# Hedgehog attention with a SwiGLU gate: the casts of wo bound behind the second query tile's exponentials, and the last wo rows in another buffer

## The chip, the cores and the metric

The kernel runs on one core of one Trainium2 chip. The metric is the device time of one execution in microseconds (us); the median of three runs is given. The engines are called as in the profile: PE is TensorE's matrix multiplication and PEld its weight load, DVE is VectorE, ACT is ScalarE, POOL is GpSimd, and SP is the sync engine, whose queue issues most of the DMAs.

## What is computed

The sequence has S = 2048 rows of D = 576; the attention has H = 32 heads of 18; the feed-forward part has F = 4608 hidden columns. Cut to what matters:

```python
xn = layernorm(x)
q, k, v = heads(xn @ wqkv)
phi(p) = concatenate([softmax(p), softmax(-p)])      # p = q @ w_phi or k @ w_phi, per head: 36 features
kv, z = phi(k)^T v, sum over the rows of phi(k)
o = (phi(q) kv) / (phi(q) z + 1e-6)
s = merged(o) @ wo
g = silu((silu(xn @ w_gate) * (xn @ w_up)) @ w_down)
out = x + s * g
```

## The kernel before, in words

All matrix products run in a reduced 32-bit format, with each fp32 operand split in a high part and a low part: the high part is a cast on ACT (`split` L58, `split_rows` L62), the low part is the source less the cast, on DVE (L59, L63, and L64 for a few leftover rows). A product of two split operands takes three matmuls per piece, high by high, high by low and low by high (`xw` L92, L614).

The program runs in stages. Up to about 230 us of the trace it normalizes x, folds w_phi into the query and key weights, and builds kv and z over the 16 row tiles. Then comes the query stage, 230 to 475 us: 16 query tiles of 128 rows in pairs. Each (`q_tile`, L558 on) multiplies xn by the query weights into a PSUM tile of two banks (`p2`, one buffer for all query tiles, 28 matmuls of 288 columns). `softmax_parts` (L272 to L286) then takes, for each sign, the maximum or minimum per head (L278) and subtracts it (L279), both on DVE; the subtractions are collected in the list `read`, the key tiles' ahead of the query tiles', so that `read[2 * NT + 1]` is the second subtraction of the first query tile and `read[-1]`, when `split_wo` runs, that of the second. ACT takes the two exponentials (L282), DVE the sums (L285). The rest of a query tile is DVE's: the product with z (`ez`, L567), its sum (L569), and small operations that end in scaling `e` in place (L577). `numer` (L579 to L597) transposes the pair of e tiles on PE, splits them and multiplies by kv; `project` (L599 to L620) multiplies by wo, whose halves are `WOH` and `WOL`, and stores s to memory (`so`, L619 and L620).

wo comes in three loads (L531) to buffers that the query stage uses later for something else: `oh`, `ol` and `ez`. `split_wo` (L533 on), which is called once, behind the first pair of query tiles, makes WOH (ACT, L58) and WOL (DVE, L59) of them.

Meanwhile PE also works on "early" tiles of the gate and up product, so that it isn't idle when the attention is: `early_weights` (L100) loads a block of weights (`raw`) and splits it (`wh`, `wl`), `early_tile` (L113) does 14 gate matmuls of 512 columns, a silu on ACT (L119), 14 up matmuls, the product h on DVE (L122) and its store (L123). A pool of PSUM tiles `pe` with two buffers holds both products. `tails` (L540 to L555) prepares the leftover weight rows: a load `tl`, four POOL subtractions (L546 to L549), a cast `th` on ACT (L550), a low part on DVE, and eight stores by POOL.

From 512 us to the end, Strassen-like products of gate and up (L707) alternate with the down products (L832). Their weights are loaded by SP (`ld`, L676), combined by POOL into `ts` and back into `ld` (L694 to L697), cast and made low by `split` into `w`, and stored for a second use (L687). ACT copies a product out of PSUM (`s` from `px`, L736); POOL and DVE combine the hidden tiles (`ha`, `hb`, `h`, L916 to L934), whose split halves `hh` enter the down products with those of the down weights (`dw`, from `rt`, `rb` and `td`).

The order of each engine's instructions is made by a scheduler from the order of the code and its priorities: what stands in `tc.high_priority()` goes first when it can, and `tc.issue_after(x)` puts what is issued in it behind instruction x, but only those of its instructions that run on x's own engine. An engine then works strictly in its order. Buffers of a pool are handed out in turn, so a tile waits until the last reader of the buffer is done.

Of the kernel before, what the change touches and what calls it, by code (L numbers as in the profile page):

```python
# [9 lines left out]
F32 = mybir.dt.float32  # L10
F32R = mybir.dt.float32r
AF = mybir.ActivationFunctionType
# [4 lines left out]
S, D, H, DH, F = 2048, 576, 32, 18, 4608  # L17
P = 128
NT = S // P
# [18 lines left out]
def heads(ap):  # L38
    return ap.rearrange("p (h d) -> p h d", d=DH)
# [7 lines left out]
def gated_hedgehog_kernel(ctx: ExitStack, tc, x, w_qk, w_v, w_phi, wo, w_gu, w_tail, w_down, ident_in, mask_in, out):  # L47
# [5 lines left out]
    nc = tc.nc  # L53
# [3 lines left out]
    def split(hi, lo, src):  # L57
        nc.scalar.copy(hi, src)  # L58
        nc.vector.tensor_sub(lo, src, hi)  # L59
# [22 lines left out]
    def xw(ps, i, j, cols, wh, wl, stationary_x):  # L82
        pairs = []
        for k in range(2):
            b = XB[i][2 * j + k]
            for c in range(2):
                pairs += [(b[:, c, cols], w[:, k, c]) for w in (wh, wl)]
                pairs += [(b[:, 3 + c, cols], wh[:, k, c])]
            pairs += [(b[0:96, 2, cols], wh[0:96, k, 2])]
        for n, (a, b) in enumerate(pairs):  # L90
            l, r = (a, b) if stationary_x else (b, a)
            last = nc.tensor.matmul(ps, l, r, start=n == 0, stop=n == len(pairs) - 1)  # L92
        return last
# [16 lines left out]
            parts.append((hi, lo))  # L110
        return parts

    def early_tile(f, i, parts, js=(0, 1), banks=None):  # L113
        for j in js:
            pg, pu = banks or [eps.tile([P, BT], F32, name="pe") for _ in range(2)]
            xw(pg, i, j, slice(0, BT), *parts[0], False)
            h = epool.tile([P, BT], F32, name="h")
            with tc.high_priority():
                nc.scalar.activation(h, pg, AF.Silu)  # L119
            last = xw(pu, i, j, slice(0, BT), *parts[1], False)  # L120
            with tc.high_priority():
                nc.vector.tensor_mul(h, pu, h)  # L122
            nc.sync.dma_start(h_dram[i, f, :, j * BT:(j + 1) * BT], h)  # L123
        return last

    with ExitStack() as att:
# [9 lines left out]
        with ExitStack() as wst:  # L136
# [129 lines left out]
            kk = kst.enter_context(tc.tile_pool(name="kk", bufs=2, side="right", reuse_waits="tile"))  # L266
# [6 lines left out]
            def softmax_parts(ps, e):  # L273
                m = kk_pool.tile([P, 2, H], F32, name="m", bufs=1)
                p4 = ps[:, :, 0:HALF].rearrange("p a (h d) -> p a h d", d=DH)
                for s, op in enumerate((ALU.max, ALU.min)):
                    m3 = m[:, s].rearrange("p (a h) -> p a h", a=2)
                    nc.vector.tensor_reduce(m3, p4, axis=AX.X, op=op)  # L278
                    read.append(nc.vector.tensor_sub(e[:, s * D:(s + 1) * D].rearrange("p (a h d) -> p a h d", a=2, d=DH),  # L279
                                                     p4, m3.unsqueeze(3).to_broadcast([P, 2, H // 2, DH])))  # L280
                for s in range(2):
                    nc.scalar.activation(e[:, s * D:(s + 1) * D], e[:, s * D:(s + 1) * D], AF.Exp,  # L282
                                         scale=1.0 if s == 0 else -1.0)
                sm = kk_pool.tile([P, 2 * H], F32, name="sm")
                nc.vector.reduce_sum(sm, heads(e), axis=AX.X)  # L285
                return sm  # L286

            kk_pool, read = kk, []

            def kv_step(n, phi, v):  # L290
                for i in range(2 * NG):
# [199 lines left out]
        with ExitStack():  # L491
# [6 lines left out]
            banks = [(i, 4 if i < 2 else 2, GROUPS[2 * i][1]) for i in range(3)]  # L498
# [23 lines left out]
        with ExitStack() as qst:  # L522
            qw = qst.enter_context(tc.tile_pool(name="qw", bufs=1, reuse_waits="tile"))
            qk = qst.enter_context(tc.tile_pool(name="qk", bufs=2, reuse_waits="tile"))
# [1 line left out]
            WOH = qw.tile([GW, NG, D], F32R, name="WOH")  # L526
            WOL = qw.tile([GW, NG, D], F32R, name="WOL")
            wrs = [qk.tile([P, 2, D], F32, name="oh", bufs=1), qk.tile([P, 2, D], F32, name="ol", bufs=1),
                   qk.tile([P, 2, D], F32, name="ez", bufs=1)]
            for g, (o, w) in enumerate(GROUPS):  # L530
                nc.sync.dma_start(wrs[g // 2][0:w, g % 2], wo[o:o + w, :])  # L531

            def split_wo():  # L533
                with tc.issue_after(read[-1].ins):
                    for n, wr in enumerate(wrs):
                        g, w = slice(2 * n, min(2 * n + 2, NG)), GROUPS[2 * n][1]
                        split(WOH[0:w, g], WOL[0:w, g], wr[0:w, 0:min(2, NG - 2 * n)])

            kk_pool = qk
# [99 lines left out]
        for f, halves in [(1, (0,)), (0, (0,))] + [(f, (1, 0)) for f in range(2, EARLY - 1)]:  # L639
            parts = first_weights.pop() if f == 1 else early_weights(f, read[2 * NT + 1] if f == 0 else None)  # L640
            for i in halves:
                early_tile(f, i, parts, (1,) if f == 1 else (0, 1))

    fw = ctx.enter_context(tc.tile_pool(name="fw", bufs=1))
    fp = ctx.enter_context(tc.tile_pool(name="fp", bufs=1, reuse_waits="tile"))
# [74 lines left out]
    def stored(src, fill):  # L720
        h = h_tile()
        for r in range(2):
            nc.sync.dma_start(h[r], src[:, r * BT:(r + 1) * BT])
        for _ in range(2):
            fill()
        return h
# [296 lines left out]
    parts = early_weights(EARLY - 1)  # L1023
# [11 lines left out]
    for i, n, f in units:  # L1035
# [9 lines left out]
        h = stored(h_dram[i, f], fill) if f < EARLY else gate_up(w, xo, fill, f - EARLY + (NF if i else 0))  # L1045
# [60 lines left out]
```

## Time and profile before

| what | value |
|---|---|
| median of 3 runs | 1640.28 us (1638.73 to 1642.0) |
| the profiled execution's own time | 1638.38 us |
| its span, first to last instruction | 1636.6 us, so 1.8 us lie around it |
| mean granted PE clock | 0.998 |
| PE busy in the span | 1604.0 us (98%) |
| DVE, ACT, POOL busy | 71%, 44%, 40% |
| instructions | 25198 |

In a row of the timeline stand the start, the busy time, the engine, the line, the operation, the tiles written and read with their shapes, the count of neighbours that were taken together, and in brackets the engine's idle time before it and what ended that. In the names the buffer numbers are left out. A row of the page's DMA table gives the count, the size of one and the time from issue to landing.

### The profile page before, as it was taken

Reading aid. Unit: us, or ns where it says so; the run is one execution under the profiler, and the core shown is the slowest. Engines: PE = TensorE matmul, PEld = TensorE weight load, DVE = VectorE, ACT = ScalarE, POOL = GpSimd, SP = SyncE. Lnnn points to the kernel's source line nnn. Section 1 sums busy time; section 2 is a strip of 40 time slices with the busy share of each in tenths; the row PEclk is TensorE's granted clock in tenths of the full one; section 3 lists DMA queues with packets and bytes.
Section 4 is the critical chain, followed back from the end, with each engine's and each line's share of the span. In section 5 each row is a group of like instructions: output and inputs, shape, how many; then the busy total and the mean of one; then the engine's idle time right before and its main releaser. Section 6 shows DMA issues by size and latency. Waiting matters only on the chain.

```text
span 1636.6 us, 25198 instructions
## 1 busy us (share of the span) xinstructions
PE 1604.0 (98%) x9385; PEld 1429.7 (87%) x9385; DVE 1168.5 (71%) x1721; ACT 721.9 (44%) x1391; POOL 653.3 (40%) x699
## 2 busy tenths in 40 slices
PE   6999998999999999999999999999999999999998
PEld 5899997999978888888888888888888888888887
DVE  7677768899952678778777778825666766666578
ACT  5533345444432554544444544455433433333334
POOL 3485661333212455455545355313233324133132
PEclk9999999999999999999999999999999999999999
DMA  9622243334248545555554554684454655555444
GB/s 286 206 80 78 85 134 117 117 103 126 67 144 306 184 165 175 179 178 168 177 180 165 175 192 152 224 296 150 136 162 135 199 184 170 172 179 185 140 115 174
DMA packets 121741, 268.46 MB, mean 164 GB/s; under 512 B 12787, under 2 KB 53363, under 8 KB 119827
## 3 DMA queue, kind: packets, MB, share of 16 engines
q1 hardware_dynamic: 106652, 246.49, 45.9%
q0 software_dynamic: 3072, 11.02, 2.4%
q10 hardware_dynamic: 11894, 9.35, 1.8%
q8 instruction: 74, 1.21, 0.3%
q14 instruction: 49, 0.39, 0.1%
HBM read 167.19 MB, written 99.61 MB: 163 GB/s over the span
## 4 chain that ended last, share of the span: by engine, by line
PE 90%; DMA 4%; DVE 3%; POOL 1%; issue 1%; ACT 1%; SPq 0%; ACTq 0%; POOLq 0%; DVEq 0%
PE px L707 24%; PE pd L832 24%; PE pw L707 12%; PE py L707 6%; PE p L92 6%; PE pe L92 5%; PE p L614 4%; PE po L594 2%; PE kvp L294 2%; PE vx L382 1%; PE pt L588 1%; DMA xn<-in_A_x 1%; PE vw L382 1%; DMA s_dram<-so 1%; DMA sraw<-in_A_w_v 1%
## 5 line engine op out<-in xcount | busy, mean ns | idle before, releaser
L832 PEld LDWEIGHTS pd<-dw,hh 128*128 128x128 f32 x3048 | 432.4, 188 | 26.4 <-DVE dw L59 1.7
L832 PE MATMUL pd<-dw,hh 128*128 128x288 f32 x3048 | 448.5, 297 | 4.3 <-DVE dw L59 1.5
L707 PE MATMUL px<-X,w 128*128 128x512 f32 x1488 | 384.3, 393 | 0.0
L707 PEld LDWEIGHTS px<-X,w 128*128 128x128 f32 x1488 | 270.6, 188 | 51.8 <-ACT s L736 2.0
L707 PE MATMUL pw<-X,w 128*128 128x512 f32 x732 | 188.7, 393 | 0.0
L707 PEld LDWEIGHTS pw<-X,w 128*128 128x128 f32 x732 | 137.0, 188 | 30.5
L741 DVE TENSOR_TENSOR s<-pw,s 128x512 f32<-128x512 f32 x124 | 85.1, 688 | 100.0 <-ACT s L736 89.2
L957 DVE TENSOR_TENSOR acc<-pd,acc 128x576 f32<-128x576 f32 x128 | 96.2, 752 | 83.8 <-PE pd L832 83.6
L736 ACT COPY s<-px 128x512 f32<-128x512 f32 x124 | 72.6, 585 | 157.2 <-PE px L707 157.2
L92 PE MATMUL pe<-X,wh 128*128 128x512 f32 (+1 forms) x380 | 121.8, 401 | 5.8 <-ACT h L119 2.9
L59 DVE TENSOR_TENSOR hh<-ha,hh 128x512 fp32r<-128x512 f32 x140 | 111.5, 823 | 20.7 <-ACT hh L58 19.1
L58 ACT CAST hh<-ha 128x512 fp32r<-128x512 f32 x140 | 82.7, 619 | 92.4 <-PE pd L832 73.5
L929 POOL TENSOR_TENSOR hb<-hb 128x512 f32<-128x512 f32 x34 | 47.0, 1381 | 168.6 <-DVE hb L753 161.4
L59 DVE TENSOR_TENSOR w<-ld,w 128x512 fp32r<-128x512 f32 (+1 forms) x93 | 77.2, 832 | 35.7 <-ACT w L58 34.5
L707 PE MATMUL px<-X,wt 96*128 96x512 f32 x248 | 97.9, 395 | 0.0
L707 PE MATMUL py<-X,w 128*128 128x512 f32 x372 | 96.5, 394 | 0.0
L916 POOL TENSOR_TENSOR h<-ha,hb 128x512 f32<-128x512 f32 x34 | 44.3, 1302 | 126.8 <-DVE ha L757 88.6
L942 POOL TENSOR_TENSOR ha<-ha 128x512 f32<-128x512 f32 x34 | 52.6, 1564 | 103.5 <-DVE hh L59 103.5
L58 ACT CAST w<-ld 128x512 fp32r<-128x512 f32 (+1 forms) x93 | 51.0, 549 | 89.6 <-POOL ld L697 56.8
L92 PEld LDWEIGHTS pe<-X,wh 128*128 128x128 f32 (+1 forms) x380 | 70.0, 189 | 21.7 <-ACT h L119 3.4
L761 ACT COPY py<-px 128x512 f32<-128x512 f32 x62 | 35.5, 572 | 102.7 <-PE px L707 80.8
L707 PEld LDWEIGHTS py<-X,w 128*128 128x128 f32 x372 | 66.7, 188 | 11.2
(262 smaller groups left out, 3199.0 us busy)
## 6 DMA issues: line engine op xcount, KB each, us to landing
w_dram<-w SPq DMA_DIRECT2D x90, 512.0 KB, 2.9
w<-w_dram SPq DMA_DIRECT2D x90, 512.0 KB, 4.5
wt<-t_dram SPq DMA_DIRECT2D x61, 336.0 KB, 3.7
ld<-in_B_w_gu SPq DMA_DIRECT2D x31, 512.0 KB, 4.5
X<-sum_dram SPq DMA_DIRECT2D x8, 1280.0 KB, 11.1
rt<-in_B_w_down SPq DMA_DIRECT2D x33, 288.0 KB, 3.1
rb<-in_B_w_down SPq DMA_DIRECT2D x33, 288.0 KB, 4.7
w_dram<-w SPq DMA_DIRECT2D x30, 256.0 KB, 2.1
```

Of the source, the lines that this page charges most:

```text
L58: nc.scalar.copy(hi, src)
L59: nc.vector.tensor_sub(lo, src, hi)
L92: last = nc.tensor.matmul(ps, l, r, start=n == 0, stop=n == len(pairs) - 1)
L614: nc.tensor.matmul(ps[:, 0:HALF], a[0:w, g, jc], bw[0:w, g, n], start=k == 0, stop=k == 3 * NG - 1)
L707: nc.tensor.matmul(ps, l, r, start=first and n == 0, stop=last and n == len(mm) - 1, skip_group_check=True)
L736: nc.scalar.copy(t, ps)
L741: nc.vector.tensor_add(t, ps, t)
L832: nc.tensor.matmul(ps, l, r, start=first and n == 0 and m == 0, stop=n == len(hs) - 1 and m == 2, skip_group_check=True)
L916: sub(s, g["h"][0][0], g["h"][0][1])
L929: nc.gpsimd.tensor_add(a21, a21, g["h"][1][1])
L942: sub(a12, a12, g["h"][0][0])
L957: nc.vector.tensor_add(a2, pd[:, :, 0:HALF], a2)
```

## The change

There are three edits. The casts of wo were bound behind `read[-1]`, the second query tile's last subtraction. That is a DVE instruction, so only the low parts were bound by it, and the casts on ACT were free. Now they are bound behind `exps[-1]`, that tile's second exponential, which is an ACT instruction; the lows follow since they read the casts. The third load of wo goes to a buffer of `e`, of which there are four, in place of the only one of `ez`. And the product h of the first early tile in this stage (f == 1) is bound behind the first query tile's second subtraction on DVE.

```diff
--- before.py
+++ after.py
@@ -110,7 +110,7 @@
             parts.append((hi, lo))
         return parts
 
-    def early_tile(f, i, parts, js=(0, 1), banks=None):
+    def early_tile(f, i, parts, js=(0, 1), banks=None, behind=None):
         for j in js:
             pg, pu = banks or [eps.tile([P, BT], F32, name="pe") for _ in range(2)]
             xw(pg, i, j, slice(0, BT), *parts[0], False)
@@ -118,8 +118,9 @@
             with tc.high_priority():
                 nc.scalar.activation(h, pg, AF.Silu)
             last = xw(pu, i, j, slice(0, BT), *parts[1], False)
-            with tc.high_priority():
-                nc.vector.tensor_mul(h, pu, h)
+            with tc.issue_after(behind.ins) if behind else ExitStack():
+                with tc.high_priority():
+                    nc.vector.tensor_mul(h, pu, h)
             nc.sync.dma_start(h_dram[i, f, :, j * BT:(j + 1) * BT], h)
         return last
 
@@ -279,13 +280,14 @@
                     read.append(nc.vector.tensor_sub(e[:, s * D:(s + 1) * D].rearrange("p (a h d) -> p a h d", a=2, d=DH),
                                                      p4, m3.unsqueeze(3).to_broadcast([P, 2, H // 2, DH])))
                 for s in range(2):
-                    nc.scalar.activation(e[:, s * D:(s + 1) * D], e[:, s * D:(s + 1) * D], AF.Exp,
-                                         scale=1.0 if s == 0 else -1.0)
+                    last = nc.scalar.activation(e[:, s * D:(s + 1) * D], e[:, s * D:(s + 1) * D], AF.Exp,
+                                                scale=1.0 if s == 0 else -1.0)
+                exps.append(last)
                 sm = kk_pool.tile([P, 2 * H], F32, name="sm")
                 nc.vector.reduce_sum(sm, heads(e), axis=AX.X)
                 return sm
 
-            kk_pool, read = kk, []
+            kk_pool, read, exps = kk, [], []
 
             def kv_step(n, phi, v):
                 for i in range(2 * NG):
@@ -526,12 +528,12 @@
             WOH = qw.tile([GW, NG, D], F32R, name="WOH")
             WOL = qw.tile([GW, NG, D], F32R, name="WOL")
             wrs = [qk.tile([P, 2, D], F32, name="oh", bufs=1), qk.tile([P, 2, D], F32, name="ol", bufs=1),
-                   qk.tile([P, 2, D], F32, name="ez", bufs=1)]
+                   qk.tile([P, 2 * D], F32, name="e", bufs=4).rearrange("p (a n) -> p a n", a=2)]
             for g, (o, w) in enumerate(GROUPS):
                 nc.sync.dma_start(wrs[g // 2][0:w, g % 2], wo[o:o + w, :])
 
             def split_wo():
-                with tc.issue_after(read[-1].ins):
+                with tc.issue_after(exps[-1].ins):
                     for n, wr in enumerate(wrs):
                         g, w = slice(2 * n, min(2 * n + 2, NG)), GROUPS[2 * n][1]
                         split(WOH[0:w, g], WOL[0:w, g], wr[0:w, 0:min(2, NG - 2 * n)])
@@ -639,7 +641,7 @@
         for f, halves in [(1, (0,)), (0, (0,))] + [(f, (1, 0)) for f in range(2, EARLY - 1)]:
             parts = first_weights.pop() if f == 1 else early_weights(f, read[2 * NT + 1] if f == 0 else None)
             for i in halves:
-                early_tile(f, i, parts, (1,) if f == 1 else (0, 1))
+                early_tile(f, i, parts, (1,) if f == 1 else (0, 1), behind=read[2 * NT + 1] if f == 1 else None)
 
     fw = ctx.enter_context(tc.tile_pool(name="fw", bufs=1))
     fp = ctx.enter_context(tc.tile_pool(name="fp", bufs=1, reuse_waits="tile"))
```

Behind the edits, lines of the new kernel stand one or two further down (L119 is still L119, L122 becomes L123, L282 L283, L550 L552, L567 L569, L676 L678). The scheduler's order changes in two places.

The first is the head of the query stage, on ACT and DVE, at some 240 to 260 us. On ACT, `e_2461` and `e_2511` are the first two query tiles, `h_4816` and `h_4850` the first two early tiles of f = 0, `wh_4869` is the cast of the next block's weights, and `th_4582` that of the first tail. Before:

```order
L282 ACTIVATE e_2461<-e_2461 128x576 x2
L58 CAST WOH_2422<-oh_2424 126x1152
L58 CAST WOH_2422<-ol_2425 126x1152
L58 CAST WOH_2422<-ez_2426 72x576
L550 CAST th_4582<-tl_4581 128x896
L282 ACTIVATE e_2511<-e_2511 128x576
L62 CAST wh_4869<-raw_4868 128x768
L119 ACT_TABLE_LOAD
L119 ACTIVATE h_4816<-pe_4800 128x512
L282 ACT_TABLE_LOAD
L282 ACTIVATE e_2511<-e_2511 128x576
```

After:

```order
L283 ACTIVATE e_2461<-e_2461 128x576 x2
L552 CAST th_4582<-tl_4581 128x896
L62 CAST wh_4869<-raw_4868 128x768
L119 ACT_TABLE_LOAD
L119 ACTIVATE h_4816<-pe_4800 128x512
L283 ACT_TABLE_LOAD
L283 ACTIVATE e_2511<-e_2511 128x576 x2
L58 CAST WOH_2422<-oh_2424 126x1152
L58 CAST WOH_2422<-ol_2425 126x1152
L58 CAST WOH_2422<-e_2426 72x576
L119 ACT_TABLE_LOAD
```

The three casts of wo went from behind the first tile's exponentials to behind the second's; the second tile's two exponentials came together, behind the first silu.

DVE in the same stretch, where `p2_2482` is the product of the second query tile, `wl_4870` the low part of `wh_4869`, before:

```order
L285 TENSOR_REDUCE sm_2469<-e_2461 128x64
L278 TENSOR_REDUCE m_2512<-p2_2482 128x32
L279 TENSOR_TENSOR e_2511<-p2_2482,m_2512 128x576
L278 TENSOR_REDUCE m_2512<-p2_2482 128x32
L279 TENSOR_TENSOR e_2511<-p2_2482,m_2512 128x576
L59 TENSOR_TENSOR WOL_2423<-oh_2424,WOH_2422 126x1152
L63 TENSOR_TENSOR wl_4870<-raw_4868,wh_4869 128x512
L64 TENSOR_TENSOR wh_4869<-raw_4868,wh_4869 32x2x128
L59 TENSOR_TENSOR WOL_2423<-ol_2425,WOH_2422 126x1152
L59 TENSOR_TENSOR WOL_2423<-ez_2426,WOH_2422 72x576
L278 TENSOR_REDUCE m_2660<-p2_2630 128x32
L567 TENSOR_TENSOR ez_2471<-e_2461,zb_2356 128x1152
```

After:

```order
L569 TENSOR_TENSOR ez_2471<-e_2461,zb_2356 128x1152
L279 TENSOR_REDUCE m_2512<-p2_2482 128x32
L571 TENSOR_REDUCE y_2473<-ez_2471 128x64
L63 TENSOR_TENSOR wl_4870<-raw_4868,wh_4869 128x512
L64 TENSOR_TENSOR wh_4869<-raw_4868,wh_4869 32x2x128
L573 SCALAR_TENSOR_TENSOR y_2473<-sm_2469,y_2473 128x32
L280 TENSOR_TENSOR e_2511<-p2_2482,m_2512 128x576
L574 TENSOR_TENSOR y_2473<-y_2473,sm_2469 128x64
L279 TENSOR_REDUCE m_2512<-p2_2482 128x32
L576 TENSOR_TENSOR den_2477<-y_2473 128x32
L280 TENSOR_TENSOR e_2511<-p2_2482,m_2512 128x576
L123 TENSOR_TENSOR h_4816<-pe_4801,h_4816 128x512
```

The first tile's ez product and its reduction went ahead, and the weights' low part, which was behind the second tile's two subtractions, now stands ahead of them.

PE follows: in the new order all 28 gate and up matmuls of h_4816 but one stand in one piece ahead of three matmuls of h_4850, and then the third tile's query product.

The second place is POOL in the first Strassen tiles, at some 530 to 548 us. `ld_5566` is a load of gate and up weights, `ts_5568` what is made of it, `td_5564` a combination of down weights. Before:

```order
L916 TENSOR_TENSOR h_5622<-ha_5398,hb_5399 128x512
L929 TENSOR_TENSOR hb_5399<-hb_5399,hb_5464 128x512
L694 TENSOR_TENSOR ts_5568<-ld_5566 128x256
L695 TENSOR_TENSOR ts_5568<-ld_5566,ts_5568 128x256
L696 TENSOR_TENSOR ld_5566<-ld_5566 128x256
L697 TENSOR_TENSOR ld_5566<-ld_5566,ts_5568 128x256
L916 TENSOR_TENSOR h_5630<-ha_5495,hb_5496 128x512
L934 TENSOR_TENSOR ha_5398<-hb_5399,ha_5398 128x512
L924 TENSOR_TENSOR td_5564<-td_5564,rb_5562 128x288
```

After:

```order
L918 TENSOR_TENSOR h_5622<-ha_5398,hb_5399 128x512
L931 TENSOR_TENSOR hb_5399<-hb_5399,hb_5464 128x512
L919 TENSOR_TENSOR td_5564<-rb_5562,rt_5560 128x288
L924 TENSOR_TENSOR rt_5560<-rt_5560 128x288
L925 TENSOR_TENSOR td_5564<-rb_5562,rt_5560 128x288
L936 TENSOR_TENSOR ha_5398<-hb_5399,ha_5398 128x512
L696 TENSOR_TENSOR ts_5568<-ld_5566 128x256
L918 TENSOR_TENSOR h_5630<-ha_5495,hb_5496 128x512
L697 TENSOR_TENSOR ts_5568<-ld_5566,ts_5568 128x256
L698 TENSOR_TENSOR ld_5566<-ld_5566 128x256
L699 TENSOR_TENSOR ld_5566<-ld_5566,ts_5568 128x256
L926 TENSOR_TENSOR td_5564<-td_5564,rb_5562 128x288
```

On POOL the operations on ld_5566 went from behind hb_5399 to behind ha_5398, with h_5630 between them, since its load moved on SP's queue (rows of SP, where `w1` and `w2` are stores of finished weights). Before:

```order
L676 DMA ld_5566<-in_B_w_gu 128x4x256
L687 DMA w_dram_72<-w2_5471 128x1024
L723 DMA ha_5463<-h_dram_69 128x512
L723 DMA hb_5464<-h_dram_69 128x512
L692 DMA wt_5467<-t_dram_73 96x896
L687 DMA w_dram_72<-w1_5488 128x512
L687 DMA w_dram_72<-w2_5480 128x1024
L687 DMA w_dram_72<-w2_5484 128x1024
L676 DMA ld_5728<-in_B_w_gu 128x4x256
```

After:

```order
L689 DMA w_dram_72<-w2_5471 128x1024
L725 DMA ha_5463<-h_dram_69 128x512
L725 DMA hb_5464<-h_dram_69 128x512
L694 DMA wt_5467<-t_dram_73 96x896
L689 DMA w_dram_72<-w1_5488 128x512
L892 DMA rb_5562<-in_B_w_down 128x576
L689 DMA w_dram_72<-w2_5480 128x1024
L689 DMA w_dram_72<-w2_5484 128x1024
L678 DMA ld_5566<-in_B_w_gu 128x4x256
L678 DMA ld_5728<-in_B_w_gu 128x4x256
```

The load of ld_5566 went from ahead of the store of w2_5471 to behind those of w2_5480 and w2_5484. In the same way the load before it, ld_5468, went behind the store of the last early tile in the query stage and three stores of weights.

## The prediction

> **What bounds the kernel now.** I read the page's busy table, its slices and the shares of its chain first, to see which engine sets the time.
>
> ```profile
> PE 1604.0 (98%) x9385; PEld 1429.7 (87%) x9385; DVE 1168.5 (71%) x1721; ACT 721.9 (44%) x1391; POOL 653.3 (40%) x699
> PE 90%; DMA 4%; DVE 3%; POOL 1%; issue 1%; ACT 1%; SPq 0%; ACTq 0%; POOLq 0%; DVEq 0%
> ```
>
> TensorE (PE) works in 98% of the span and holds 90% of the chain that ended last. An edit on ScalarE (ACT), VectorE (DVE) or GpSimd (POOL) is therefore worth only what it takes from, or adds to, PE's idle time. The instruction orders of the two kernels differ only from the start of the query stage to the first Strassen tiles, 240 to 548 us of this trace; ahead of and behind that each engine runs the same sequence. So I looked at the busy time by stretch (the stretch's length, then PE, PEld, DVE, ACT and POOL, clock, DMA share, GB/s).
>
> ```profile
> 235.00:270.00 35.00, 31.20 (x156) 25.65 (x154) 26.17 (x41) 21.96 (x25) 11.40 (x20) 1.00 0.58 186
> 300.00:350.00 50.00, 50.00 (x342) 45.77 (x341) 45.36 (x70) 23.79 (x41) 16.92 (x36) 1.00 0.34 106
> 470.00:490.00 20.00, 17.93 (x94) 14.25 (x93) 7.94 (x11) 7.04 (x15) 7.32 (x8) 1.00 0.72 238
> 538.00:550.00 12.00, 9.39 (x51) 7.90 (x50) 8.92 (x13) 6.61 (x13) 6.52 (x6) 1.00 0.34 129
> ```
>
> PE idles 3.8 us at the head of the query stage, 2.1 us at its tail and 2.6 us in the first Strassen tiles; in the middle it is never idle, with DVE close behind (45.36 of 50). Those 8.5 us are about all that reordering can win. The third view, PE's timeline with its waits, names what ends each idle time.
>
> ```profile
> 255.40 0.50 PE L92 MATMUL pe<-X,wh 128*128 128x512 f32 x1 [1.19 <-ACT h L119]
> 260.49 0.50 PE L92 MATMUL pe<-X,wh 128*128 128x512 f32 x1 [1.55 <-DVE h L122]
> 270.36 0.37 PE L92 MATMUL p<-QH,X 128*128 128x288 f32 x1 [1.42 <-DVE e L279]
> 485.39 0.50 PE L92 MATMUL pe<-X,wh 128*128 128x512 f32 x1 [0.28 <-ACT h L119]
> 489.57 0.47 PE L92 MATMUL pe<-X,wh 128*128 128x512 f32 x1 [0.63 <-ACT h L119]
> 540.20 0.53 PE L832 MATMUL pd<-dw,hh 128*128 128x288 f32 x2 [1.10 <-DVE hh L59]
> 542.23 1.33 PE L832 MATMUL pd<-dw,hh 128*128 128x288 f32 x8 [1.50 <-DVE dw L59]
> 548.23 1.56 PE L707 MATMUL px<-X,w 128*128 128x512 f32 x6
> ```
>
> **Head of the query stage: the casts of wo move.** In before, ACT holds the casts of wo ahead of everything else here.
>
> ```profile
> 244.86 1.16 ACT L58 CAST WOH<-oh 126x1152 fp32r<-126x1152 f32 x1 [3.99 <-DMA oh<-in_A_wo]
> 248.05 1.16 ACT L58 CAST WOH<-ol 126x1152 fp32r<-126x1152 f32 x1 [2.04 <-DMA ol<-in_A_wo]
> 249.12 0.66 ACT L58 CAST WOH<-ez 72x576 fp32r<-72x576 f32 x1
> 251.19 0.94 ACT L550 CAST th<-tl 128x896 fp32r<-128x896 f32 x1 [1.41 <-POOL tl L549]
> 252.04 0.68 ACT L282 ACTIVATE e<-e 128x576 f32<-128x576 f32 x1
> 252.62 0.82 ACT L62 CAST wh<-raw 128x768 fp32r<-128x768 f32 x1
> 253.46 1.28 ACT L119 ACT_TABLE_LOAD   x1
> 254.75 0.60 ACT L119 ACTIVATE h<-pe 128x512 f32<-128x512 f32 x1
> ```
>
> The three casts, 1.16 + 1.16 + 0.66 = 2.98 us, leave this place. But ACT doesn't come any earlier to the silu (L119) that PE waits for: the next instruction in both orders is the cast of the first weight tail (th), and it starts at 251.19 because POOL's last subtraction on the loaded tail ends there. That load is issued ahead of the first place where the sync queue differs, so it lands at the same time. In the changed order ACT simply idles from 240.9 to 251.2. Then come th to 252.04, wh to 252.86, a table load to 254.15, the silu to about 254.75, a second load, then both exponentials of the second tile. The silu wins only the 0.6 us of the exponential that stood ahead of it.
>
> DVE pays for that. In before the second tile's two subtractions are done long before this.
>
> ```profile
> 245.06 0.76 DVE L279 TENSOR_TENSOR e<-p,m 128x576 f32<-128x576 f32 x1
> 245.73 0.75 DVE L278 TENSOR_REDUCE m<-p 128x32 f32<-128x576 f32 x1
> 246.51 0.76 DVE L279 TENSOR_TENSOR e<-p,m 128x576 f32<-128x576 f32 x1
> 253.47 0.69 DVE L63 TENSOR_TENSOR wl<-raw,wh 128x512 fp32r<-128x512 f32 x1 [4.94 <-ACT wh L62]
> 254.18 0.42 DVE L64 TENSOR_TENSOR wh<-raw,wh 32x256 fp32r<-32x256 f32 x1
> 257.24 1.34 DVE L567 TENSOR_TENSOR ez<-e,zb 128x1152 f32<-128x1152 f32 x1
> ```
>
> In the changed order the low part wl (L63), which waits for the cast wh at 252.86, stands ahead of both. So: wl and its small companion to 254.0, a subtraction to 254.8, a reduce to 255.5, the second subtraction to about 256.4 instead of 247.27. The two-bank PSUM tile of the query product is single-buffered, so the third tile's product must wait for that second subtraction. PE's order changes accordingly: it runs the 27 gate and up matmuls of the first early tile straight on, 27 x 0.234 us from 244.02 to 250.4, then waits 4.3 us for the silu, runs three matmuls, waits some 1.0 us more for the subtraction, and goes on with the third query product at 256.5. In return the first tile's ez product and its reduction (1.34 us each) stand in DVE's idle time ahead of the wait, the casts and lows of wo run behind the second tile's exponentials beside PE's 28 x 0.134 = 3.8 us of product, and the later waits of 1.55 and 1.42 us go: by the same step-by-step sum DVE has the third tile's subtractions done by 272.1, before PE wants the bank at 272.65. The sum is 1.19 + 1.55 + 1.42 = 4.16 us of idle time before against 4.3 + 1.0 = 5.3 and a few tenths after, less about 0.6 us of matmuls that run at better pace without the interruptions: **+0.6 us**. The bounds are 0 (the chain keeps PE no longer than before) and +1.6 (none of the later waits' gain beyond the first is kept).
>
> [...] ACT's next instruction starts within 0.02 us of a table load (253.46 + 1.28, then 254.75), and the cast ahead of the load ends 0.02 us before it. [...]
>
> **The wo rows in an e place.** The third load of wo took the ez buffer, of which there is one; the first ez product had to wait for its low (L59). That is the 1.34 us at 257.24, and its move is in the sum above. The e place comes back when the fourth query tile needs it, some 15 us after the lows of wo are done, so nothing waits: 0, at worst one DVE instruction of 0.75 us.
>
> **The product behind the first tile's subtractions.** In before it already stands behind them on DVE, and in the new order the same: 0. Its bounds are 0 on both sides, as the order doesn't move there.
>
> **The middle, 275 to 470 us.** The queue of ready work on DVE and ACT is shuffled, but PE is 50.00 of 50 us busy: 0. DVE's slack is 4.6 us in 50, so I bound it at 2.5 us either way.
>
> **Tail of the query stage.** The last silus wait 0.28 and 0.63 us for ACT, behind casts for the first Strassen weights (with the refill about 1.2 us of PE). In the new order the second of these silus stands right behind its weights' cast: **-0.6**, between -1.2 and 0.
>
> **The first Strassen tiles.** Here the new order moves loads on the sync queue (SP).
>
> ```profile
> 507.42 0.55 SPq L676 DMA_DIRECT2D ld<-in_B_w_gu  x1
> 522.23 0.55 SPq L676 DMA_DIRECT2D ld<-in_B_w_gu  x1
> 532.35 0.55 SPq L676 DMA_DIRECT2D ld<-in_B_w_gu  x1
> ```
>
> The page's table of DMA issues gives their median time to landing.
>
> ```profile
> ld<-in_B_w_gu SPq DMA_DIRECT2D x31, 512.0 KB, 4.5
> ```
>
> The load at 507.42 goes behind the last early store and three weight stores, to about 515, and lands (4.5 us) near 520, just when ACT's cast of it is due: **+0.5**, between 0 and 2. The load at 522.23 goes to the place of the one at 532.35, so it lands at about 537.4. That frees the lows on which PE waits at 540.20 and 542.23, and holds up the four POOL operations on the loaded weights.
>
> ```profile
> 538.38 2.37 DVE L59 TENSOR_TENSOR hh<-ha,hh 128x512 fp32r<-128x512 f32 x2
> 540.67 1.51 DVE L59 TENSOR_TENSOR dw<-rt,dw 128x288 fp32r<-128x288 f32 x1
> 542.10 1.28 DVE L59 TENSOR_TENSOR hh<-h,hh 128x512 fp32r<-128x512 f32 x2
> 543.31 0.45 DVE L59 TENSOR_TENSOR dw<-td,dw 128x288 fp32r<-128x288 f32 x1
> 533.84 0.74 POOL L695 TENSOR_TENSOR ts<-ld,ts 128x256 f32<-128x256 f32 x1
> 534.53 1.25 POOL L696 TENSOR_TENSOR ld<-ld 128x256 f32<-128x256 f32 x1
> 540.22 1.64 POOL L934 TENSOR_TENSOR ha<-hb,ha 128x512 f32<-128x512 f32 x1 [0.63 <-DVE hh L59]
> 547.16 0.58 ACT L736 COPY s<-px 128x512 f32<-128x512 f32 x1
> ```
>
> The lows hh and dw come some 2.4 us sooner, and of PE's 3.0 us (1.10 and 1.50 with their refills) about 0.5 is left. But the weights' last two casts now wait for POOL at about 543.6, and behind them on ACT the copy s of px ends at about 548.4, not 547.74. PE, which would reach its next px matmul at 548.23 - 2.4 = 545.8, starts it at about 548.5: the gain is given back, **+0.2**, between -2.4 and +1.0 (POOL's four operations at 0.74 or all at 1.25).
>
> **Sum.** 0.6 - 0.6 + 0.5 + 0.2 = +0.7 us on the profiled execution's own 1638.38 (its span of 1636.6 and 1.8 around it), or 1639.1. The median of the three runs, 1640.28, lies 1.9 above that execution, so I forecast 1640.28 + 0.7 = **1641.0**, with 1638 to 1644 as this case's own range. About 0.2%, 3.3 us, is what a measurement of this kernel can tell from no change.
>
> **Rivals.**
> Slower, by collision on DVE and POOL at 538 to 548 us. The same two lows take 2.37 us beside POOL's h and ha operations and 1.28 without; a dw low takes 1.51 beside POOL's ha, which ends at 541.86, and 0.45 alone. The moved POOL operations now stand among the lows. If they collide, DVE loses 1.09 + 1.06 = 2.1 us and POOL 4 x (1.25 - 0.74) = 2.0, in one chain to the copy s; it decides as soon as s ends later than 548.23, which the forecast already has. That gives 1641.0 + 4.1 = 1645.1. For it speaks that POOL's row of 1.25 lies in the same stage; against it that DVE idles in most of these 12 us. [...]
>
> Faster: both tails clear. If the copy s isn't late, the whole 2.4 us stay won, the silus' 1.2 us go, and the head costs 0: 1640.28 - 3.6 = 1636.7. For it speaks that PE's waits there have names that the new order serves earlier; against it the later load.
>
> The change doesn't do what it says: the second tile's exponentials come to stand at about 256 us, against 252.04 and 256.66 for the two in before, since both hang on the tail's load rather than on wo. If in addition the rest of the order has no effect, the time is 1640.3.
>
> **How the numbers follow.** Forecast 0.48, collision 0.29, both tails clear 0.18, no effect 0.05. Faster by over 0.2% means below 1637.0: the clear case's 0.18 and 0.02 of the forecast, for a middle that gains its whole 2.5 us, 0.20. Slower means above 1643.6: 0.26 of the collision's 0.29 (the rest is a collision in part) and 0.04 of the forecast's upper edge, 0.30. Within is what is left, 0.42 + 0.03 + 0.05 = 0.50. The range takes in the clear case at 1636.7 less a little of the middle, and the collision at 1645.1 with the head's upper bound of 1.0 more: 1636.0 to 1646.5.
>
> **What would show it.** At the head: an idle ACT up to the cast of th at 251.2, the second subtraction at about 256.4, and one PE wait of some 4 us in place of 1.19, 1.55 and 1.42. At the first Strassen tiles: no wait of PE for hh and dw, the loads at about 515 and 532, and a px that waits for ACT's copy s. The prediction is wrong if the tail lands at another time, if PE gets idle time between 275 and 470 us, or if PE's px at 548 starts at once.

## The result, and the profile after

| | before | changed |
|---|---|---|
| median of 10 runs | 1638.76 us (1635.62 to 1642.0) | 1643.97 us (1640.98 to 1646.27) |
| ratio, 95% interval | | 1.0032 (1.0024 to 1.0041) |
| the profiled execution, and its span | 1638.38 us, 1636.6 us | 1645.06 us, 1643.3 us |
| mean granted PE clock of the profiled execution | 0.998 | 0.996 |

The change makes the kernel slower by 5.2 us (3.9 to 6.7). The two profiled executions lie 6.7 us apart, but 2.3 us of that arise before the first changed instruction: the silu that precedes the query stage starts at 236.98 in before and at 239.32 in the changed kernel. In the twelve profiles that silu starts between 235.28 and 239.32, without order by the edits, so this is spread between executions. Times of the changed profile are therefore read against before's plus 2.3 at the head, and, since the last early silu stands at 509.51 and 513.12, plus 3.6 at the first Strassen tiles. At the end of those tiles (the pd group of 549.86 before, 555.73 after) the distance is 5.9.

The busy time by stretch, for the same stretches as before (PE, PEld, DVE, ACT, POOL, clock, DMA share, GB/s):

```profile
235.00:270.00 35.00, 30.39 (x149) 25.69 (x148) 24.39 (x36) 17.11 (x21) 13.52 (x22) 0.90 0.51 166
300.00:350.00 50.00, 50.00 (x339) 45.87 (x338) 42.37 (x68) 24.42 (x42) 21.01 (x41) 1.00 0.40 117
470.00:490.00 20.00, 19.98 (x126) 17.03 (x124) 8.00 (x14) 7.38 (x14) 0.00 (x0) 1.00 0.20 63
538.00:550.00 12.00, 10.83 (x58) 9.21 (x56) 8.53 (x11) 4.30 (x8) 7.68 (x8) 1.00 0.65 207
```

The column to look at is the clock: at the head it fell from 1.00 to 0.90. The third row ends ahead of a wait of 1.01 us for ACT's copy so at 491.17 (in before 1.17 us at 477.94), and the last row ends inside the second wait below, so their PE columns aren't to be compared with before's. PE's timeline shows the slower clock in the matmuls themselves.

```profile
257.26 0.79 PE L92 MATMUL pe<-X,wh 128*128 128x512 f32 x1 [4.43 <-ACT h L119]
257.85 0.63 PE L92 MATMUL pe<-X,wl 128*128 128x512 f32 x1
258.28 0.63 PE L92 MATMUL pe<-X,wh 128*128 128x512 f32 x1
259.09 0.58 PE L92 MATMUL p<-QH,X 128*128 128x288 f32 x1 [0.18 <-DVE e L280]
552.68 2.93 PE L709 MATMUL px<-X,w 128*128 128x512 f32 x6 [3.85 <-ACT s L738]
555.40 0.48 PE L709 MATMUL px<-X,wt 96*128 96x512 f32 x1
```

Two long waits, 4.43 us for the silu and 3.85 us for ACT's copy s, and a short one of 0.18 us have taken the place of the seven that the prediction lists for before. Behind each long one, matmuls take nearly twice their time: six of 512 columns 2.93 us, where before has 1.56. The head's chain on ACT and DVE ran in the order that was foreseen:

```profile
253.63 0.94 ACT L552 CAST th<-tl 128x896 fp32r<-128x896 f32 x1 [10.42 <-POOL tl L551]
254.47 0.83 ACT L62 CAST wh<-raw 128x768 fp32r<-128x768 f32 x1
256.61 0.60 ACT L119 ACTIVATE h<-pe 128x512 f32<-128x512 f32 x1
552.05 0.57 ACT L738 COPY s<-px 128x512 f32<-128x512 f32 x1
```

```profile
255.33 0.70 DVE L63 TENSOR_TENSOR wl<-raw,wh 128x512 fp32r<-128x512 f32 x1 [5.44 <-ACT wh L62]
258.19 0.76 DVE L280 TENSOR_TENSOR e<-p,m 128x576 f32<-128x576 f32 x1
543.78 2.94 DVE L59 TENSOR_TENSOR hh<-h,hh 128x512 fp32r<-128x512 f32 x2
```

ACT is idle for 10.42 us up to th; then th, wh, a table load and the silu, and on DVE wl ahead of the second subtraction. Divided into pieces of 3.4 us, the same profile shows how clock and idle time hang together (0.50 in the clock's column, the third number from the end, is what I call half clock):

```profile
251.80:255.20 3.40, 1.03 (x5) 0.50 (x3) 0.00 (x0) 1.57 (x2) 3.08 (x8) 1.00 0.58 227
255.20:258.60 3.40, 1.34 (x3) 0.83 (x3) 3.22 (x8) 3.34 (x5) 3.40 (x8) 0.50 0.50 82
258.60:262.00 3.40, 3.22 (x13) 2.94 (x13) 3.37 (x6) 3.40 (x5) 0.92 (x2) 0.50 0.95 351
262.00:265.40 3.40, 3.40 (x25) 3.22 (x24) 3.40 (x4) 1.73 (x2) 0.00 (x0) 0.99 0.08 32
548.80:552.20 3.40, 0.03 (x1) 0.00 (x0) 1.65 (x5) 2.21 (x6) 1.00 (x2) 1.00 0.55 164
552.20:555.60 3.40, 2.92 (x7) 2.34 (x8) 3.40 (x4) 2.15 (x5) 2.71 (x3) 0.50 0.84 308
555.60:559.00 3.40, 3.40 (x22) 3.08 (x21) 0.76 (x2) 1.23 (x2) 0.00 (x0) 1.00 0.76 241
```

The trace's clock records change only at multiples of 3.413 us from one another; the pieces are laid on that grid. A piece in which PE was busy for 1.03 of 3.40 us is followed by one at half clock; that one, itself idle for the most part, by another; a busy one ends it. In the slow pieces PE worked 1.34 + 3.22 and 2.92 us, and half of that, 2.3 and 1.5 us, is my estimate of what the clock took. The second place bears it out: from the px group to the pd group behind it PE took 3.05 us (552.68 to 555.73), in before 1.63 (548.23 to 549.86), so 1.4 more.

### The profile page after: what moved, and what is told of

Read it like the earlier page. It is cut to its first block, busy times and chain, and to the rows that moved or that the text cites. A ratio compares the mean times of both kernels' runs of the same rounds, so it can differ in the third digit from the quotient of the medians.

```text
span 1643.3 us, 25199 instructions
## 1 busy us (share of the span) xinstructions
PE 1605.5 (98%) x9385; PEld 1432.0 (87%) x9385; DVE 1168.9 (71%) x1721; ACT 721.5 (44%) x1391; POOL 656.0 (40%) x699
## 4 chain that ended last, share of the span: by engine, by line
PE 64%; DVE 1%; DMA 1%; issue 0%; POOL 0%; ACT 0%; SPq 0%; ACTq 0%; DVEq 0%
PE pd L834 23%; PE px L709 23%; PE pw L709 11%; PE py L709 6%; DVE acc L806 0%; DMA rb<-in_B_w_down 0%; DVE w L59 0%; DMA X<-s_dram 0%; DVE hh L59 0%; DVE acc L807 0%; DVE s L743 0%; DVE acc L991 0%; DVE ha L759 0%; POOL hb L931 0%; ACT w L58 0%
```

## The experiments

I began with this theory: the e place alone moves the work that costs, and PE's idle time costs itself and, above some length (I first took the 3.41 us of a stretch, which no run had shown), half clock behind it. The rivals were that the moved casts cost, that the waits alone cost, and that DVE and POOL collide at the first Strassen tiles whatever the load does. Each kernel was timed beside before in five rounds, but for the probe, which was run once. The ratios are to the before of the same rounds, so kernels of different rounds are best compared by them.

**The casts alone** (casts_only): only `exps` and the binding of `split_wo`.

```diff
-                with tc.issue_after(read[-1].ins):
+                with tc.issue_after(exps[-1].ins):
```

> The casts of wo bound behind the exponentials; the last rows of wo stay in the ez place. Theory A (the place is what costs: it lets the first ez product go early, by which the weights' low part comes to stand ahead of the second tile's subtractions, and it moves the load at the first Strassen tiles; PE idles over 3.4 us at both places and then runs at half clock): here PE's order at the head is that of before, so no idle time over 2 us, no half clock behind the start of the program, and 1636 to 1641 us, within 0.15% of before. Rival B (the casts are what costs, as ACT then idles until the weight tail's cast): an idle time of PE of 4 us at the head as in the changed kernel, and 3 to 5 us over before.

Measured 1640.73 us, ratio 1.0011 (1.0001 to 1.0020). PE's waits at the head are for the same three things as in before (0.81, 1.71 and 1.12 us), and no stretch is at half clock. So the casts are not what costs 5 us. The 1.9 us that they do cost lie within what I expected. Where they arise isn't shown: the profiled execution took 1638.22 us, 2.5 under the median. It has one wait of over 1 us in a place where before has none, 1.25 us for ACT's copy py at 526 us, since in this order too the load of the third block of gate and up weights goes behind the last early stores.

**The place alone** (place_only).

```diff
-                   qk.tile([P, 2, D], F32, name="ez", bufs=1)]
+                   qk.tile([P, 2 * D], F32, name="e", bufs=4).rearrange("p (a n) -> p a n", a=2)]
```

> The last rows of wo in an e place; the casts stay bound as before. Theory A: all of the change's cost: a PE wait of some 4.4 us for the silu at the head and of some 3.9 us for ACT's copy at the first Strassen tiles, half clock behind each, and 1642 to 1645 us, 0.2 to 0.4% over before. Rival B: near before, 1637 to 1640 us, with no wait over 2 us at the head.

Measured 1643.78 us, ratio 1.0031 (1.0020 to 1.0041): as much as all of the change. But the head is not the changed kernel's, and the wait of 4.4 us that I expected isn't there. Without the third edit DVE takes the early product h ahead of the first query tile's subtractions; in before and in the changed kernel it stands behind them (there 242.66, the second subtraction 238.29):

```profile
240.72 0.69 DVE L122 TENSOR_TENSOR h<-pe,h 128x512 f32<-128x512 f32 x1 [5.86 <-PE pe L92]
241.33 0.75 DVE L279 TENSOR_TENSOR e<-p,m 128x576 f32<-128x576 f32 x1
```

That the place alone costs as much as the whole change is therefore in part a coincidence, and neither the third edit alone nor the two others without it were run. The wait for ACT's copy s at the first Strassen tiles did come, with 3.04 us. The head of this profile also refutes the length that I had assumed. PE's waits there:

```profile
241.56 0.47 PE L92 MATMUL pe<-X,wh 128*128 128x512 f32 x1 [0.70 <-DVE h L122]
243.68 0.37 PE L92 MATMUL p<-QH,X 128*128 128x288 f32 x1 [1.65 <-DVE e L279]
255.79 0.51 PE L92 MATMUL pe<-X,wh 128*128 128x512 f32 x1 [0.54 <-ACT h L119]
257.64 0.37 PE L92 MATMUL p<-QH,X 128*128 128x288 f32 x1 [1.35 <-DVE e L279]
```

and its stretches, with the clock again the third number from the end:

```profile
241.50:244.90 3.40, 1.69 (x10) 1.44 (x11) 3.35 (x6) 0.58 (x1) 0.00 (x0) 1.00 0.88 265
244.90:248.30 3.40, 3.40 (x16) 3.40 (x15) 0.81 (x3) 3.15 (x5) 0.00 (x0) 0.50 0.90 261
255.10:258.50 3.40, 1.50 (x8) 1.07 (x8) 3.40 (x9) 3.34 (x6) 2.97 (x7) 1.00 0.91 227
258.50:262.00 3.50, 3.50 (x17) 3.50 (x16) 3.50 (x4) 1.10 (x1) 0.00 (x0) 0.51 0.64 232
```

No wait is longer than 1.65 us, and still two stretches are at half clock: each follows one in which PE was busy for less than half (1.69 and 1.50 of 3.40). In casts_only the least busy stretch of the head stays above it, by little, and nothing follows:

```profile
256.10:259.50 3.40, 1.74 (x8) 1.08 (x6) 3.22 (x4) 3.38 (x5) 0.00 (x0) 1.00 0.53 215
259.50:262.90 3.40, 3.35 (x14) 2.74 (x15) 3.40 (x4) 3.36 (x5) 0.00 (x0) 1.00 0.22 80
```

**The tail's cast later** (tail_cast_late): the changed kernel, one ACT instruction moved.

```diff
-                nc.scalar.copy(hi, t)
+                with tc.issue_after(exps[NT + 1].ins) if n == 0 else ExitStack():
+                    nc.scalar.copy(hi, t)
```

> The changed kernel with one instruction moved: the cast of the first weight tail goes behind the second query tile's exponentials. Theory A: the silu no longer waits for POOL and starts when the weights' cast is done, some 2 us sooner; PE's wait falls from 4.4 to about 2.4 us, under the 3.4 us, so no half clock follows at the head: 2.0 us of idle time and 2.2 to 2.4 us of slow matmuls gone, 1639 to 1640.5 us. Rival C (the half clock has nothing to do with the idle time; only the wait counts): 2.0 us gone, 1642 us, and a half-clock stretch at the head as before. The wait at the first Strassen tiles stays in both.

Measured 1643.6 us, ratio 1.0029 (1.0017 to 1.0040): nothing gained that can be told from the spread, and both numbers of mine were wrong. The cast of the weights, next in line, waits for its own load. It starts at 250.72; in the changed kernel it started at 254.47, or 251.4 less the 3.0 us by which this execution is ahead at the silu before. So it came only 0.7 us sooner:

```profile
250.72 0.83 ACT L62 CAST wh<-raw 128x768 fp32r<-128x768 f32 x1 [10.54 <-DMA raw<-in_B_w_gu]
```

```profile
253.51 0.51 PE L92 MATMUL pe<-X,wh 128*128 128x512 f32 x1 [3.71 <-ACT h L119]
```

PE's wait shrank from 4.43 to 3.71 us and the clock fell for two stretches as before (0.51 and 0.50). Behind one late transfer stood another, and the wait was now for that one.

**The load early** (load_early): the changed kernel, one load put ahead on the sync queue, PE's order untouched.

```diff
-            nc.sync.dma_start(ld, w_gu[f, :, :, 0:2])
+            with tc.high_priority() if f == EARLY + 3 else ExitStack():
+                nc.sync.dma_start(ld, w_gu[f, :, :, 0:2])
```

> The changed kernel with one load of gate and up weights put back early on the sync queue; PE's order is that of the changed kernel. Theory A: the wait of 3.85 us for ACT's copy of px at 552 us goes with the half clock behind it (1.4 us), and the waits for hh and dw of before (2.6 us) partly come back: 2.5 to 4 us less, 1640 to 1641.5 us. Rival D (the collision of DVE and POOL costs there whatever the load): a wait of PE of over 3 us stays, less than 1.5 us gained, 1642.5 to 1644 us. The head's wait and half clock stay in both.

Measured 1641.63 us, ratio 1.0021 (1.0012 to 1.0029), 2.3 us under the changed kernel's median. By the ratios the gain is 1.8 us, and the intervals of the two overlap. The profile is clearer. The wait for ACT's copy s is gone, the waits for hh and dw are back at 0.79 and 1.64 us, and no half clock follows; the least busy stretch there keeps 1.76 us of work:

```profile
542.40:545.80 3.40, 1.76 (x12) 1.57 (x12) 3.40 (x4) 0.30 (x1) 2.74 (x3) 1.00 0.87 311
545.80:549.20 3.40, 3.40 (x18) 2.90 (x17) 1.88 (x4) 1.81 (x5) 0.81 (x1) 1.00 0.01 5
```

Against the rival, the late load is what cost there. The gain lies just under what I expected (2.5 to 4). The head's wait (3.85 us) and its half clock (0.51 and 0.50 in the two stretches behind it) stay, as expected.

**The weights later** (weights_late): the changed kernel with tail_cast_late's edit, and the next block's weight cast behind the first silu.

```diff
-                nc.scalar.activation(h, pg, AF.Silu)
+                silus.append(nc.scalar.activation(h, pg, AF.Silu))
...
-                    split_rows(hi, lo, raw)
+                    with tc.issue_after(silus[-2].ins) if f == 2 else ExitStack():
+                        split_rows(hi, lo, raw)
```

> The changed kernel with the cast of the first weight tail behind the second query tile's exponentials and the next block's weight cast behind the first silu; by it the weights' low part goes behind the second tile's subtractions on DVE, PE runs 21 matmuls of the third query product right behind 26 of the early tile, and the load of gate and up weights at the first Strassen tiles comes back to its early place. Theory A (the time is lost where PE waits for ACT and DVE behind transfers, and where a stretch with half its time idle is followed by half clock): no wait over 2 us at the head, no half clock, tail as in before: 1636 to 1639.5 us. Rival E (the e place itself costs, by the early ez product on DVE and the e buffers that come round one tile sooner): 1641 to 1644 us with waits spread over the query stage.

Measured 1636.46 us, ratio 0.9994 (0.9983 to 1.0005): all 5 us come back, with the e place and the moved casts still in. So against the rival the place needn't cost; what cost was the order that came with it, weights that wait for a load ahead of the silu and of the subtractions. With that order the load at the first Strassen tiles comes early again too, and the wait for ACT's copy s is gone. I had expected no wait over 2 us at the head; one of 2.70 us is left, with a stretch of half clock (its matmuls of 288 columns start 0.24 us apart, those ahead of the wait 0.13):

```profile
254.04 0.66 PE L594 MATMUL pt<-ident,e 128*126 128x128 f32 x2 [2.70 <-ACT WOH L58]
```

In this profile the clock also fell once at the first Strassen tiles, on the two waits that before has too:

```profile
537.13 0.53 PE L838 MATMUL pd<-dw,hh 128*128 128x288 f32 x2 [0.70 <-DVE hh L59]
539.17 1.45 PE L838 MATMUL pd<-dw,hh 128*128 128x288 f32 x8 [1.51 <-DVE dw L59]
540.42 2.76 PE L713 MATMUL py<-X,w 128*128 128x512 f32 x6
```

Here the second and the end of the first fell into one stretch (1.66 us of work in 3.40); in before's profile 1.10 and 1.50 fell into two, and the clock stayed. The probe below, in which PE's order is that of before, has 0.87 and 1.50 us there, 2.02 us of them in one stretch, and half clock behind it. The grid lies differently in each of the twelve profiles, and between its first record (at 14 to 17 us) and 230 us, where PE's order is the same in all, six have no stretch at half clock, four have one and two have two. So the same order costs a half-clock stretch in some executions and not in others, which is a part of the runs' spread.

**The casts and the weights later** (casts_weights_late): the casts' edit without the place, and both edits of weights_late.

> Only the casts of wo bound behind the exponentials (the ez place kept), with the cast of the weight tail behind the second tile's exponentials and the next block's weight cast behind the first silu; PE's order is that of before. Theory A: the silu starts when its product is done, so the wait of 1.19 us at the head goes; the waits for the product h (1.55) and the subtraction (1.42) stay or shrink: 1636.5 to 1639.5 us, 0.5 to 2 us less than the casts alone. Rival F (what the casts alone cost, 1.9 us, is given by the shuffled middle and the first Strassen tiles, not by the head): within 1 us of the casts alone, 1640 to 1641.5 us.

Measured 1636.99 us, ratio 0.9996 (0.9985 to 1.0006): 3.7 us under casts_only's median and 2.5 by the ratios, more than the 0.5 to 2 expected. PE's waits at the head are 0.38 and 1.11 us, and no stretch is at half clock.

**The probe** (probe_waits): before, with copies ahead of the silus of the last four early tiles; the copies are overwritten by the silu.

```diff
             with tc.high_priority():
+                for _ in range({(1, 0): 8, (1, 1): 9, (0, 0): 10, (0, 1): 12}[i, j] if f == EARLY - 1 else 0):
+                    nc.scalar.copy(h, pg)
                 nc.scalar.activation(h, pg, AF.Silu)
```

> The kernel before with 8, 9, 10 and 12 copies of the gate product put ahead of the silu in the last four early tiles, so that PE waits for the silu by some 1.6, 2.1, 2.7 and 3.7 us, once per 7 to 10 us, in a stretch in which it is otherwise busy. Theory A (the clock for a stretch of 3.41 us is set by how much of the stretch before it was idle, about half of it or more giving half clock): half clock behind the last two waits at least, and behind the second if it falls into one stretch; 8 to 10 us of waiting and 3 to 6 us of slow matmuls, 1649 to 1656 us. Rival G (only an idle time longer than 3.41 us does it): half clock behind the last wait alone. Rival C (waits have nothing to do with it): no half clock there.

Measured 1660.37 us, above the range: the waits were 1.90, 2.98, 3.60 and 4.59 us, longer than planned. The first, spread over two stretches, left the clock alone; the three others lowered it:

```profile
494.20:497.60 3.40, 2.17 (x9) 1.81 (x10) 0.69 (x1) 1.14 (x2) 0.00 (x0) 1.00 0.99 365
501.10:504.50 3.40, 1.14 (x5) 0.56 (x3) 0.00 (x0) 3.24 (x6) 0.00 (x0) 1.00 0.94 319
504.50:507.90 3.40, 2.69 (x6) 2.17 (x7) 0.69 (x1) 0.63 (x2) 0.00 (x0) 0.50 0.99 334
507.90:511.30 3.40, 3.40 (x9) 2.67 (x8) 0.00 (x0) 0.00 (x0) 0.00 (x0) 0.50 0.96 354
```

The wait of 2.98 us is shorter than a stretch and still brought two at half clock. So the clock follows the waits also where they are put in a place that had none, and no wait has to fill a stretch.

**Towards a faster kernel.** casts_weights_late_load is casts_weights_late with load_early's edit for `f == EARLY + 2`; weights_late_only is before with only the two weight edits; weights_late_load is weights_late with the load's edit.

> The kernel of casts_weights_late with the load of the third block of gate and up weights issued sooner on the sync queue, ahead of the last four early tiles' stores. Theory A (idle time of PE is what counts, one for one, and more where it fills half of a stretch): the wait of 1.1 us for ACT's copy py at 524 us goes, and nothing else moves: 1635 to 1636.5 us, 0.15 to 0.2% under before. Rival H (the wait moves to the next transfer): within 0.5 us of casts_weights_late, 1637 us.

> The kernel before, with neither the casts of wo moved nor the place; only the cast of the weight tail goes behind the second query tile's exponentials, and the next block's weight cast behind the first silu. If the casts of wo ahead of the exponentials cost what the change's author meant to save, the silu here still waits for the loads of wo: a wait at the head of about 0.5 us for the silu, and h and the subtraction as in before: 1638 to 1639 us. If they cost nothing once the weight casts are out of the way: as casts_weights_late, 1636.5 to 1637.5 us, and the rest of the gain is the weights' alone.

> The kernel of weights_late (all of the change, with the weight casts later) with the load of the third block of gate and up weights issued sooner. Theory A: the wait of 1.1 us for py goes, the head's wait of 2.7 us with its half clock stays: 1635 to 1636 us. Rival H: within 0.5 us of weights_late, 1636.5 us.

Measured 1636.04 us, ratio 0.9984 (0.9976 to 0.9993); 1636.48 us, 0.9985 (0.9977 to 0.9994); and 1637.0 us, 0.9984 (0.9974 to 0.9993). All three are faster than before by intervals that leave out 1, by 0.15%, and can't be told from each other. The third lies 1 us above what I expected of it; its wait for py is gone and the head's wait (2.19 us), with half clock behind it (matmuls of 288 columns 0.24 us apart), stays, as expected. The second has no wait for the silu at the head, where one of 0.5 us was possible. In the first the wait for py is gone, as the list of PE's waits between 225 and 580 us shows (us in total, times, longest):

```profile
PE pd L838 <- DVE dw L59: 1.5, 1, 1.5
PE p L92 <- DVE e L282: 1.1, 1, 1.1
PE p L619 <- ACT so L624: 0.9, 2, 0.7
PE pd L838 <- DVE hh L59: 0.7, 1, 0.7
PE px L713 <- ACT s L742: 0.3, 1, 0.3
```

weights_late_only gains as much with none of the change in it, so the gain is the weight casts'. Whether the load's edit adds anything stays open: the two pairs differ by less than their intervals.

## Why the prediction was right in its range, and what it missed

The forecast was 1641.0 with 1636.0 to 1646.5; it came to 1643.97, slower by over 0.2%, which had 0.30. That it lies so near is in part luck. The three runs of before that the forecast started from had a median 1.5 us above that of the ten; as a change, +5.2 us stands against +0.7. And the range reached as far up for a collision of DVE and POOL; half clock behind a wait is in none of the cases.

- **What bounds the kernel, and where the orders differ.** Held. From 275 to 470 us PE is busy 194.95 of 195 us, in before 194.98: the middle brought no idle time.
- **The head's waits.** Held in mechanism and size: ACT idle up to th, the silu, 2.3 us of shift aside, from 254.3 to 254.9 (forecast: done at about 254.75), a wait of 4.43 us (4.3). The second wait, for the subtraction, is 0.18 and not 1.0 us, because the three matmuls ahead of it ran at half clock (1.65 us, from 257.26 to 258.91; in before three of the same kind took about 0.97 behind the wait at 255.40).
- **The head's sum, +0.6: the step that failed.** The term took the 5.3 us of waiting as idle time alone and had PE go on "at 256.5" at full pace. By the times between matmuls, PE lost 7.1 us from 250 to 275 where before lost 5.1: +2.0, above the term's bound of +1.6. The difference is the 2.3 us that the half clock took, less the 0.8 us by which the second wait was shorter.
- **The tail of the query stage, -0.6.** Held: both waits for the silu are gone. Head, middle and tail together moved the last early silu by 3.61 - 2.34 = 1.3 us, so the tail and the middle gave 0.7.
- **The first Strassen tiles, +0.5 and +0.2: mis-sized.** The +0.5 for the first load came to nothing: PE has no wait from 512 to 548 us. The waits for hh and dw went and a late copy s came, as forecast. Shifted by 3.6, PE was ready at 545.2 (forecast 545.8) and the copy ended at 549.0 (548.4): the wait was 3.85 us and not 2.7. Then came the half clock, 1.4 to 1.5 us. Measured over the stage: 5.9 - 3.6 = +2.3.
- **The collision.** It was there in part: the lows hh take 2.94 us beside POOL, where before's took 1.28 with POOL idle. Its share in the 0.6 us by which the copy came later isn't separated, since the load itself came late: issued at 533.1, the shift aside (forecast 532.35), it was waited for until 538.9 (landing forecast at about 537.4). load_early shows that the late load made the loss; more than half of the loss was the clock's.
- **The rest.** Half clock, 2.3 + 1.5 = 3.8 us by estimate, is the term that the forecast of +0.7 lacks. The two make 4.5, where the profiled pair shows 3.6 us in the changed stages: the second wait at the head was shorter by 0.8. Another 0.8 arises behind the changed stages, and nothing explains it; nor does the pair explain the 1.6 us from 3.6 to the medians' 5.2. The other runs of the changed kernel had lower clocks than its profiled one (0.9951 on the mean, against 0.9962; one stretch at half clock takes 0.001 off), which points the right way, but their traces weren't kept.

Before's profile alone hardly gives the step: its clock is 1.00 in each stretch that the prediction shows, with a single slow stretch near the start (at 18.9 us, behind one in which PE worked 1.67 of 3.50 us), and its longest wait at the head is 1.55 us. The runs give it: between 228 and 578 us a stretch that was less than half busy was enough, and in place_only a wait of 1.65 us with the last 0.08 us of another did it (1.69 us of work in 3.40).

## What to carry to other kernels

A wait of PE isn't priced one for one: when a reordering gathers several short waits into one long one, ask what share of a 3.4 us stretch it leaves busy. Between 228 and 578 us of the twelve profiles, each of the 15 stretches in which PE waited for 1.72 us or more at full clock was followed by one at half clock (0.50); half of the work in that one is my estimate of the cost. At the head the waits' sum rose only from 4.16 to 4.61 us, and PE lost 2.0 us more. And look at which instruction stands, in its engine's order, ahead of the one that PE waits for (in the changed kernel ACT idled 10.42 us up to th, and the silu, behind it, came 14.7 us after the start of the first tile's exponentials, 256.61 after 241.95; in weights_late, where th and wh come behind the silu, 7.7 us, 245.56 after 237.91). Moving two weight casts, which waited for their loads, from ahead of the exponentials and the silu to behind them gained 2.2 us in the kernel before (1636.48 against 1638.67 us). There the casts' edit and the place's each lost time.

## What the runs showed of the hardware

I divided the twelve profiles between 228 and 578 us into stretches of 3.413 us, on each execution's grid of clock records: 1216 in all, 1197 of them at full clock. In 15 of these PE waited for 1.72 us or more, and each is followed by a stretch at half clock; in the other 1182 it waited for 1.68 us at most, and none is. Here the border lies between 1.68 and 1.72 us, about half of the stretch (1.71). Of the 19 at half clock, those with up to 0.51 us of waiting (15) are followed by full clock, those with 0.69 us or more (4) by another at half. From 578 to 1620 us no stretch is at half clock. Near the program's start the border is less sharp: in casts_weights_late a stretch with 1.76 us of waiting, at 29.5, left the clock at full, and in weights_late_load one with 1.38 us, at 32.1, was followed by half clock. What the clock counts as busy isn't shown; the waits are those that the profile names.
